# The second pointwise product of a conformer block: twelve of sixteen chunks by Strassen's seven products, with row sums on GpSimd

## The chip, the cores and the metric

The kernel runs on one core of one Trainium2 chip. The metric is the device time of one execution in microseconds; lower is better. The engines of a core are called by their names in the profile: PE (TensorE, with PEld for its weight loads), DVE (VectorE), ACT (ScalarE), POOL (GpSimd) and SP (SyncE, which issues most of the transfers).

## The reference

A conformer block over x of shape 2 x 4000 x 512 in bfloat16: a feed-forward layer, attention, a convolution module, a second feed-forward layer, with layer norms between. The part around the change is the end of the convolution module and what follows it.

```python
B, T, D = x.shape
...
h = _layernorm(x2, axis=-1)
h = h @ w_pw1
a = h[..., :D].copy()
b = h[..., D:].copy()
h = a * _sigmoid(b)
...                       # depthwise convolution over 3 tokens: dc
flat = dc.reshape(-1, D)
mu = flat.mean(0)
var = ((flat - mu) ** 2).mean(0)
dc = (dc - mu[None, None, :]) / jnp.sqrt(var[None, None, :] + 1e-05)
h = _silu(dc) @ w_pw2     # the second pointwise product
x3 = x2 + h
h = _layernorm(x3, axis=-1)
h = _silu(h @ w_ff2_a) @ w_ff2_b
x4 = x3 + 0.5 * h
return _layernorm(x4, axis=-1)
```

The second pointwise product multiplies each token's 512 values by the 512 x 512 matrix w_pw2, and its result is added to x2.

## The kernel before, in words

The tokens are worked on in 16 chunks (NCK) of up to 512, eight for each of the two sequences (TCB); the eighth of each has 416. A chunk has four token tiles of up to 128. The norm over all tokens inside the convolution module cuts the work in two: what follows it, called the second stage here, can start only when the convolution of all chunks is done. The second stage is a loop over c = 0 to 14 (`ff2`) and a last piece for chunk 15 (`ff_last`).

`ff2(c)` runs the second feed-forward layer of chunk c in 16 steps f (`ff_chunk`). Its two matrix products are done by Strassen's scheme, with matmuls of 128x256. Beside each step, `hook(f)` lays work for the chunks ahead: for chunk n = c + 2 (AHEAD is 2) the second pointwise product, for chunk n + 1 the silu that feeds it (`swish`, on ACT, into one of two buffers z), and the load of an x chunk (`get_x`). Layer norms of chunk c + 1 ("in") and of chunk c ("out") run as jobs beside them: statistics on DVE, a power on POOL, a small product on DVE, and the scaling on ACT.

The second pointwise product before is plain. At the steps f = 6, 8, 10 and 12 (8, 10, 12, 14 for c = 0) one token tile is done: `pw2` issues four matmuls of 128x512, one for each 128 of the 512 inputs, which add up in a bank of PSUM. Two steps later `pw2_residual` adds the bank to x in SBUF by one DVE scalar_tensor_tensor (xt<-y,xt in the profile). The bank comes from `sbank`, which is bank 7 in this stage. The results wait in x for the layer norm.

The x of a chunk lives in one of six homes of 4096 bytes per partition, called slots (SLOTS), and one chunk has a home of its own (TCB - 1). `slot(c, by)` names the home; `get_x` issues its load on SP's queue. The output of a chunk is stored from its home, also on SP's queue, and the home can be loaded again when that store is done. Before, `get_x(n + 1, ...)` stands at f = 8.

The order of the instructions on each engine is not the order of the code. The program collects its operations in a plan (`S.planned(16000, 8000)`), which holds costs for each operation and places them by a list schedule; `carry_out` then issues them engine by engine in that order. Almost all operations go through one helper, so the profile gives nearly all of them the same line, L93; they are told apart by engine, operation, tile names and shape. The tiles are named by their region: `xt` holds the x homes, `work`, `sums`, `keys` and `wff` are regions of SBUF with several uses each, `y` and `s` are banks of PSUM.

Of the kernel before, what the change touches and what calls it, by code (L numbers as in the profile page):

```python
# [5 lines left out]
F32 = mybir.dt.float32  # L6
BF16 = mybir.dt.bfloat16
I32 = mybir.dt.int32
ALU = mybir.AluOpType
# [6 lines left out]
TILE = 128  # L16
TPC = 4
CHUNK = TPC * TILE
# [3 lines left out]
NCK = B * TCB  # L22
# [7 lines left out]
HC, HD, HF = CHUNK // 2, D // 2, FC // 2  # L30
# [14 lines left out]
def token_tiles(c):  # L45

    return TPC if c < NCK - 1 else TPC - 1
# [510 lines left out]
class Conformer:  # L558
# [20 lines left out]

    IN = (1, 1, 2, 2, 3, 5, 5, 7, 9, 11)  # L580
    OUT = (5, 5, 9, 9, 10, 12, 13, 15, 17, 19)
    SOON = (5, 5, 9, 9, 10, 12, 12, 13, 14, 15)

    def __init__(self, nc, ins, out):
# [9 lines left out]
    def memory(self):  # L594
# [9 lines left out]
        E = Region(nc, "sums", 35840)  # L604
# [46 lines left out]
        at = [8192 + t % self.CONV_SLOTS * 4096 if t < self.NBESIDE else 20480 + (t - self.NBESIDE) * 4096  # L651
              for t in range(NCK)]
# [23 lines left out]
        def take(n):  # L676
# [6 lines left out]
                    for s in range(2)]  # L683
# [97 lines left out]
        self.b_zh = [[[C.buf("zh", o + cc * 2 * CHUNK + h * 2 * HC, 2 * HC) for h in range(2)] for cc in range(DC)]  # L781
                     for o in (oM, oQ0)]
        assert off[0] == 47104

        homes = ((C, oQ1), (E, 28672), (W, 8192))
        self.h2 = [[R.view(o + j * 1024, D) for j in range(TPC)] for R, o in homes]
# [1790 lines left out]
    def pw2(self, t, tiles, banks, start=True):  # L2577

        for ccs in (range(1), range(1, 2), range(2, 3), range(3, DC)) if len(tiles) > 1 else (range(DC),):
            for ti, (ps, b_ps) in zip(tiles, banks):  # L2580
                for cc in ccs:
                    self.mm(ps[0:TILE, :], self.z[t % 2][:, cc, ti * TILE:(ti + 1) * TILE], self.Wp2[:, cc, :],
                            start and cc == 0, cc == DC - 1,
                            [self.b_z[t % 2][cc] if t > 1 else self.b_zh[t][cc][ti // 2], self.b_Wp2], b_ps, inc=cc == ccs[-1])

    def pw2_residual(self, t, tiles, banks):
        for ti, (ps, b_ps) in zip(tiles, banks):
            self.residual(ps[0:TILE, :], b_ps, t * TPC + ti, 1.0)
# [53 lines left out]
    def program(self, any_score):  # L2642
# [50 lines left out]
        def ff1(c):  # L2693
# [26 lines left out]
            def done():  # L2720
                self.put_x(c)
                late = (self.SOON, (1, 1, 1, 1, 2, 2, 3, 3, 4, 4) if not any_score else (2, 2, 3, 3, 4, 6, 6, 6, 7, 7), (18, 18, 19, 19, 20, 22, 22, 23, 24, 25))
                self.ln_job(c, "key", "ACT", self.OUT if c < NCK - 3 else late[c - NCK + 3])

# [170 lines left out]
        x = [(ps[0:TILE, :], b_ps) for ps, b_ps in banks]  # L2895
# [8 lines left out]
        for k in range(2):  # L2904
# [3 lines left out]
            for ti in pair:  # L2908
# [3 lines left out]
                                                            in1=self.neghalf[0:TILE, two], op=ALU.pow),  # L2912
                 reads=self.b_mv[sl][two] + [self.b_neghalf], writes=self.b_rs[sl][two])
            S.op("DVE", lambda e, two=two: e.scalar_tensor_tensor(
                out=self.sh[sl][:, two], in0=self.mv[sl][:, two, 0], scalar=-1.0, in1=self.rs[sl][:, two],
# [8 lines left out]
        for h in range(2):  # L2924
            for f, (ps, b_ps) in enumerate(self.early):
                out = ps[:, h * HC:(h + 1) * HC].rearrange("p (t k) -> p t k", t=2)
                for cc in range(DC):
                    self.mm(out, self.Wa[:, cc, f * 128:(f + 1) * 128], self.lnT[0][:, 2 * h:2 * h + 2, cc, 0:TILE],
                            cc == 0 and h == 0, cc == DC - 1, [self.b_Wa[f * self.NWA // FC]] + self.b_lnT[0][2 * h:2 * h + 2],
                            b_ps, skip_group_check=True)  # L2930
        for ti in all_t:
            ps, b_ps = banks[ti]
            self.away("ACT", self.XT[ti], ps[0:TILE, :], b_ps, [self.bx[ti]], self.b_lnT[0])

        def ff2(c):
            def hook(f):
                n = c + AHEAD
                if f == 8 and n + 1 < NCK:
                    self.get_x(n + 1, self.slot(n + 1, 2))
                if c == 0 and f < 2:  # L2940
                    self.fetch_conv(3 + f)
                if c == 0 and f == 0:
                    for cc in range(DC):
                        self.swish(1, cc, 1, behind=self.b_lnT[0][0:1])
                if c == 0 and f in (2, 4):
                    ti = 1 + f // 2
                    bank = [self.sbank()]
                    self.pw2(1, [ti], bank)
                    self.after(1, lambda: self.pw2_residual(1, [ti], bank))
                if c == 0 and f in (2, 3, 5, 6):  # L2950
                    self.swish(n, (2, 3, 5, 6).index(f), behind=self.b_lnT[0][2:4])
                if c == 0 and f == 7:
                    self.fetch_conv(5)
                at = (8, 10, 12, 15) if c == 0 else (1, 5, 9, 13)
                if n + 1 < NCK and f in at:
                    self.swish(n + 1, at.index(f))
                if f == FC - 1 and c + 6 < self.NBESIDE:
                    self.fetch_conv(c + 6)
                times = (8, 10, 12, 14) if c == 0 else (6, 8, 10, 12)
                if n < NCK and f in times[0:token_tiles(n)]:  # L2960
                    ti = times.index(f)
                    bank = [self.sbank()]
                    self.pw2(n, [ti], bank)
                    self.after(2, lambda: self.pw2_residual(n, [ti], bank))
                if f == 0 and c + 1 < NCK:
                    if c:
                        self.ln_job(c + 1, "in", "ACT", self.IN)
                    else:
                        self.ln_job(1, "in", "ACT", (3, 4, 5, 7, 7, 8, 8, 8, 9, 9))

            def done():
                if c < NCK - 2:
                    self.ln_job(c, "out", "ACT", self.OUT)
                else:
                    self.ln_job(c, "out")

            self.ff_chunk(c, second, hook, done)

        self.fast, self.mixed = [c < NCK - 1 for c in range(NCK)], True
# [63 lines left out]
```

## Time and profile before

| | |
|---|---|
| median of 3 runs | 1875.03 us (1874.97 to 1876.97) |
| the profiled execution's own time | 1876.08 us |
| its span, first to last instruction | 1871.9 us |
| granted TensorE clock | 0.999 |
| PE busy | 1851.6 us (99%) |
| DVE busy | 1471.1 us (79%) |
| ACT busy | 1317.5 us (70%) |
| POOL busy | 135.4 us (7%) |
| second stage, steady chunks | about 1484 to 1791 us of the span |

Busy time is the time in which at least one instruction of the engine was running; for PE the ends of matmuls are modelled, since they overlap. The difference between the profiled execution's time and its span is what lies before the first and after the last instruction. A row of a group reads: line, engine, operation, written tile from read tiles, shape, count, then busy time and mean duration in ns, then the idle time of the engine just before these instructions and what ended most of it. A row of the timeline reads: start, duration, engine, line, operation, and in brackets the idle time before it.

### The profile page before, as it was taken

The page shows a single profiled execution, that of the slowest core. Times are in us where ns is not written, and L with a number is a line of the kernel's source. Part 1 is how long each engine was busy: PE and PEld are TensorE (multiplying, and loading weights), DVE is VectorE, ACT ScalarE, POOL GpSimd, SP SyncE. Part 2 cuts the span into 40 slices and gives each one's busy share as a digit, 9 for nine tenths or more (in the row PEclk, how much of TensorE's full clock was granted, in tenths as well). Part 3 has the DMA queues.
Part 4 walks back from the last instruction along what each step waited for, and adds up shares of the span by engine and source line. Part 5 has one row for each costly group of instructions (what it writes and reads, how often), then busy time and mean ns, then how long its engine had stood idle before and what let it go on. Part 6 is the DMA issues. An engine that isn't in the chain of part 4 may idle for free.

```text
span 1871.9 us, 39333 instructions
## 1 busy us (share of the span) xinstructions
PE 1851.6 (99%) x15370; PEld 1453.3 (78%) x15484; DVE 1471.1 (79%) x3212; ACT 1317.5 (70%) x2441; POOL 135.4 (7%) x302
## 2 busy tenths in 40 slices
PE   9999999999999999999999999999999999999998
PEld 6888888866777777777677777777775888888886
DVE  8888888868767777776777677767778988888875
ACT  6877777644666777777667676777668787777773
POOL 1000000000000000000000001000011000000000
PEclk9999999999999999999999999999999999999999
DMA  7333344297545555447955444444365222212111
GB/s 197 85 90 91 80 113 107 53 261 224 177 142 146 164 170 162 112 137 170 231 150 142 124 123 111 125 137 122 109 206 163 83 57 73 75 46 62 49 43 33
DMA packets 325014, 231.53 MB, mean 124 GB/s; under 512 B 204179, under 2 KB 295638, under 8 KB 324566
## 3 DMA queue, kind: packets, MB, share of 16 engines
q1 hardware_dynamic: 324294, 228.68, 44.4%
q8 instruction: 124, 2.03, 0.4%
q14 instruction: 68, 0.56, 0.1%
q10 hardware_dynamic: 528, 0.26, 0.0%
HBM read 128.44 MB, written 55.79 MB: 98 GB/s over the span
## 4 chain that ended last, share of the span: by engine, by line
PE 93%; DVE 2%; ACT 2%; DMA 1%; issue 1%; SPq 1%; DVEq 0%
PE y L93 48%; PE s L93 45%; ACT sums L93 1%; DVE work L93 1%; DVE xt L93 1%; SPq L93 1%; ACT work L93 0%; DMA kfd<-xt 0%; DVE sums L93 0%; DMA vhd<-wff 0%; DVE wff L93 0%; ACT wff L93 0%; ACT keys L93 0%; DMA wff<-keysd 0%; DMA work<-work 0%
## 5 line engine op out<-in xcount | busy, mean ns | idle before, releaser
L93 ACT ACTIVATE sums<-s 128x512 bf16<-128x512 f32 (+3 forms) x501 | 290.4, 584 | 112.2 <-PE s L93 108.4
L93 ACT ACTIVATE keys<-s 128x512 bf16<-128x512 f32 (+2 forms) x271 | 158.7, 588 | 176.0 <-PE s L93 158.1
L93 DVE TENSOR_TENSOR sums<-sums 128x512 bf16<-128x512 bf16 (+3 forms) x528 | 195.8, 397 | 67.8 <-ACT sums L93 62.8
L93 PE MATMUL y<-work,keys 128*128 128x256 bf16 x1920 | 244.2, 273 | 0.0
L93 PE MATMUL s<-work,keys 128*128 128x256 bf16 (+5 forms) x1430 | 219.8, 290 | 2.0 <-ACT sums L93 0.3
L93 ACT ACTIVATE work<-xt,work 128x512 bf16<-128x512 bf16 x268 | 208.0, 786 | 8.1 <-DVE work L93 7.9
L93 PE MATMUL y<-sums,keys 128*128 128x256 bf16 (+1 forms) x1440 | 212.3, 270 | 0.1
L93 PE MATMUL y<-wff,keys 128*128 128x256 bf16 (+2 forms) x1590 | 208.7, 276 | 0.4 <-DVE xt L93 0.4
L93 PE MATMUL s<-sums 128*128 128x256 bf16 x1380 | 206.1, 273 | 0.8 <-DVE sums L93 0.6
L93 PEld LDWEIGHTS y<-work,keys 128*128 128x128 bf16 x1920 | 187.8, 98 | 23.5 <-DVE work L93 0.2
L93 PE MATMUL y<-work,wff 128*128 128x256 bf16 (+3 forms) x1168 | 196.1, 291 | 0.0
L93 DVE TENSOR_TENSOR keys<-keys 128x1024 bf16<-128x1024 bf16 (+2 forms) x262 | 168.9, 663 | 27.9 <-ACT keys L93 14.7
L93 PEld LDWEIGHTS y<-wff,keys 128*128 128x128 bf16 (+1 forms) x1592 | 151.2, 98 | 31.5 <-issue 3.3
L93 DVE BATCH_NORM_STATS2 work<-xt 128x6 f32<-128x512 bf16 x251 | 163.8, 679 | 1.9 <-DMA xt<-in_x_dram 1.1
L93 PEld LDWEIGHTS s<-work,keys 128*128 128x128 bf16 (+1 forms) x1456 | 118.1, 97 | 56.0 <-ACT sums L93 5.9
L93 PEld LDWEIGHTS y<-sums,keys 128*128 128x128 bf16 x1440 | 137.1, 98 | 27.6 <-issue 6.1
L93 PEld LDWEIGHTS s<-sums 128*128 128x128 bf16 x1380 | 134.6, 98 | 23.9 <-DVE sums L93 0.8
L93 POOL TENSOR_TENSOR work<-work 128x4 f32<-128x4 f32 (+3 forms) x107 | 90.0, 842 | 806.8 <-DVE work L93 804.2
L93 PE MATMUL y<-sums,xt 128*128 128x256 bf16 (+1 forms) x960 | 146.2, 270 | 0.0
L93 PEld LDWEIGHTS y<-work,wff 128*128 128x128 bf16 x1168 | 113.0, 98 | 25.8 <-ACT s L93 0.4
L93 PE MATMUL s<-xt,keys 128*128 128x256 bf16 (+1 forms) x816 | 124.3, 270 | 0.8 <-DVE xt L93 0.7
L93 PE MATMUL s<-work 128*128 128x512 bf16 (+5 forms) x494 | 118.7, 376 | 5.3 <-DVE work L93 1.4
(143 smaller groups left out, 3227.4 us busy)
## 6 DMA issues: line engine op xcount, KB each, us to landing
xt<-kfd SPq DMA_DIRECT2D x98, 384.0 KB, 3.3
xt<-v12d SPq DMA_DIRECT2D x105, 256.0 KB, 2.7
xd<-xt SPq DMA_DIRECT2D x28, 512.0 KB, 2.9
xt<-xd SPq DMA_DIRECT2D x28, 512.0 KB, 4.3
out_dram<-xt SPq DMA_DIRECT2D x14, 512.0 KB, 3.1
xt<-in_x_dram SPq DMA_DIRECT2D x13, 512.0 KB, 4.4
dcvd<-wff SPq DMA_DIRECT2D x48, 128.0 KB, 2.1
keys<-dcvd SPq DMA_DIRECT2D x12, 512.0 KB, 3.7
```

The lines of the kernel that those rows point to most:

```text
L93: return getattr(eng, self.name)(*self.args, **self.kw)
```

## The change

For the chunks n = 3 to 14 (c = 1 to 12) the product of the chunk's 512 x 512 block with w_pw2 is done by the seven products of Strassen's scheme in its Winograd form, with blocks of 256 x 256, instead of eight.

- Each of the seven products is four matmuls of 128x256 into bank 7 (`pw2_unit`), at the steps f = 3, 5, 6, 8, 9, 11 and 13 (SEVEN). One DVE tensor_tensor one step later adds the bank to a block of x, or to a partial sum in 32-bit floats (`zt`), and writes either. Three of the seven start a bank afresh; four add to what the bank already holds, so some products accumulate across units.
- The four sums of rows (tokens) of z are POOL tensor_tensor operations of 128x512 in bfloat16, at f = 0 to 3 (`pw2_sums`); three go to new buffers `zs`, one overwrites a block of z.
- The four sums of weights are made once, at c = 0 and f = 12 to 15, by DVE operations of 128x512 (`pw2_weights`), and kept in `wz`.
- `wz` takes the place of the sixth home of x. In the second stage x goes through five homes (`slot(n, 2, 5)`), and `get_x(n, ...)` stands at f = 3 of the loop that also does the product of n, where it was at f = 8 of the loop before.
- Chunks 0, 1, 2 and 15 keep the plain product.

```diff
+    SEVEN = (3, 5, 6, 8, 9, 11, 13)
...
+        at = (self.SLOTS - 1) * 4096
+        self.wz = [self.XR.view(at + m * 1024, 512).rearrange("p (c d) -> p c d", c=2) for m in range(4)]
...
+    def pw2_weights(self, step):
+        (b11, b12), (b21, b22) = [[self.Wp2[:, 2 * k:2 * k + 2, e * HD:(e + 1) * HD] for e in range(2)] for k in range(2)]
...
+        out, x, y, op, rd, wr = ((t1, b12, b11, ALU.subtract, [], n1), (t3, b22, b12, ALU.subtract, [], n3),
+                                 (t2, t3, b11, ALU.add, n3, n2), (t4, b21, t2, ALU.subtract, n2, n4))[step]
+        self.S.op("DVE", lambda e: e.tensor_tensor(out=out, in0=x, in1=y, op=op), reads=rd + [self.b_Wp2], writes=wr)
+
+    def pw2_sums(self, t, step):
...
+        out, x, y, op, rd, wr = ((s1, a21, a22, ALU.add, b_z, n1), (s2, s1, a11, ALU.subtract, n1 + b_z[0:2], n2),
+                                 (s4, a12, s2, ALU.subtract, n2 + b_z[2:4], n4),
+                                 (a21, a11, a21, ALU.subtract, b_z[0:2], b_z[0:2]))[step]
+        self.S.op("POOL", lambda e: e.tensor_tensor(out=out, in0=x, in1=y, op=op), reads=rd, writes=wr)
+
+    def pw2_unit(self, t, n):
...
+        (form, b_f), (w, b_w), new, (x, b_x), (out, b_out) = (
+            (a12, b21, True, x11, p), (a11, b11, True, p, x11), (s2, t2, False, x12, p), (s3, t3, False, x22, q),
+            (a22, t4, False, x21, x21), (s1, t1, True, q, x22), (s4, b22, False, p, x12))[n]
+        ps, b_ps = self.bank(7)
+        for u in range(2):
+            for j in range(2):
+                self.mm(ps[0:TILE, u * HD:(u + 1) * HD], form[:, j, u * TILE:(u + 1) * TILE], w[:, j, :],
+                        new and u == 0 and j == 0, u == 1 and j == 1, b_f + [b_w], b_ps, skip_group_check=True)
+        y = ps[0:TILE, :].rearrange("p (t d) -> p t d", t=2)
+
+        def add():
+            self.S.op("DVE", lambda e: e.tensor_tensor(out=out, in0=y, in1=x, op=ALU.add), reads=[b_ps] + b_x, writes=b_out)
+
+        self.after(1, add)
...
                 n = c + AHEAD
-                if f == 8 and n + 1 < NCK:
-                    self.get_x(n + 1, self.slot(n + 1, 2))
+                if f == 3 and 0 < c and n < NCK:
+                    self.get_x(n, self.slot(n, 2, self.SLOTS - 1))
+                if c == 0 and f >= 12:
+                    self.pw2_weights(f - 12)
+                seven = 0 < c and n < NCK - 1
+                if seven and f < 4:
+                    self.pw2_sums(n, f)
+                if seven and f in self.SEVEN:
+                    self.pw2_unit(n, self.SEVEN.index(f))
...
-                if n < NCK and f in times[0:token_tiles(n)]:
+                if n < NCK and not seven and f in times[0:token_tiles(n)]:
```

More of the change, by code (lines that the diff above doesn't have):

```diff
@@ L783, in memory @@
         assert off[0] == 47104
+        self.zs = [E.view(28672 + m * 1024, 512).rearrange("p (c k) -> p c k", c=2) for m in range(3)]
+        self.b_zs = [E.buf("zs", 28672 + m * 1024, 1024) for m in range(3)]
+        self.zt = [E.view(31744 + m * 2048, CHUNK, F32).rearrange("p (t d) -> p t d", t=2) for m in range(2)]
+        self.b_zt = [E.buf("zt", 31744 + m * 2048, 2048) for m in range(2)]
+        at = (self.SLOTS - 1) * 4096
+        self.wz = [self.XR.view(at + m * 1024, 512).rearrange("p (c d) -> p c d", c=2) for m in range(4)]
+        self.b_wz = [self.XR.buf("wz", at + m * 1024, 1024) for m in range(4)]
         homes = ((C, oQ1), (E, 28672), (W, 8192))
@@ L2584, in pw2 @@
                             [self.b_z[t % 2][cc] if t > 1 else self.b_zh[t][cc][ti // 2], self.b_Wp2], b_ps, inc=cc == ccs[-1])
+    def pw2_weights(self, step):
+        (b11, b12), (b21, b22) = [[self.Wp2[:, 2 * k:2 * k + 2, e * HD:(e + 1) * HD] for e in range(2)] for k in range(2)]
+        t1, t2, t3, t4 = self.wz
+        n1, n2, n3, n4 = [[b] for b in self.b_wz]
+        out, x, y, op, rd, wr = ((t1, b12, b11, ALU.subtract, [], n1), (t3, b22, b12, ALU.subtract, [], n3),
+                                 (t2, t3, b11, ALU.add, n3, n2), (t4, b21, t2, ALU.subtract, n2, n4))[step]
+        self.S.op("DVE", lambda e: e.tensor_tensor(out=out, in0=x, in1=y, op=op), reads=rd + [self.b_Wp2], writes=wr)
@@ new lines, in pw2_sums @@
+    def pw2_sums(self, t, step):
+        z, b_z = self.z[t % 2], self.b_z[t % 2]
+        (a11, a12), (a21, a22) = [[z[:, 2 * k:2 * k + 2, h * HC:(h + 1) * HC] for k in range(2)] for h in range(2)]
+        s1, s2, s4 = self.zs
+        n1, n2, n4 = [[b] for b in self.b_zs]
+        out, x, y, op, rd, wr = ((s1, a21, a22, ALU.add, b_z, n1), (s2, s1, a11, ALU.subtract, n1 + b_z[0:2], n2),
+                                 (s4, a12, s2, ALU.subtract, n2 + b_z[2:4], n4),
+                                 (a21, a11, a21, ALU.subtract, b_z[0:2], b_z[0:2]))[step]
+        self.S.op("POOL", lambda e: e.tensor_tensor(out=out, in0=x, in1=y, op=op), reads=rd, writes=wr)
@@ new lines, in pw2_unit @@
+    def pw2_unit(self, t, n):
+        z, b_z = self.z[t % 2], self.b_z[t % 2]
+        (a11, a12), (s3, a22) = [[(z[:, 2 * k:2 * k + 2, h * HC:(h + 1) * HC], b_z[2 * k:2 * k + 2]) for k in range(2)]
+                                 for h in range(2)]
+        b11, b21, b22 = [(self.Wp2[:, 2 * k:2 * k + 2, e * HD:(e + 1) * HD], self.b_Wp2) for k, e in ((0, 0), (1, 0), (1, 1))]
+        s1, s2, s4 = [(x, [b]) for x, b in zip(self.zs, self.b_zs)]
+        t1, t2, t3, t4 = zip(self.wz, self.b_wz)
+        (x11, x12), (x21, x22) = [[(self.XTc[t][:, 2 * h:2 * h + 2, e * HD:(e + 1) * HD], self.bx[t * TPC + 2 * h:t * TPC + 2 * h + 2])
+                                   for e in range(2)] for h in range(2)]
+        p, q = [(x, [b]) for x, b in zip(self.zt, self.b_zt)]
+        (form, b_f), (w, b_w), new, (x, b_x), (out, b_out) = (
[10 more added lines that the diff above has]
+        self.after(1, add)
```

## The prediction

> **What bounds the kernel now.** The page comes first: the busy times by engine, and the chain that ended last.
>
> ```profile
> span 1871.9 us, 39333 instructions
> ...
> PE 1851.6 (99%) x15370; PEld 1453.3 (78%) x15484; DVE 1471.1 (79%) x3212; ACT 1317.5 (70%) x2441; POOL 135.4 (7%) x302
> ...
> PE 93%; DVE 2%; ACT 2%; DMA 1%; issue 1%; SPq 1%; DVEq 0%
> ```
>
> TensorE (PE) is busy nearly always and carries 93% of the chain. But a share over the whole span says little about one stage, so the second look is at the stage that is changed: the chain in order of time there, whose columns are start, duration, what.
>
> ```profile
> 1511.88 1.69 PE y L93 x11
> ...
> 1539.79 1.68 PE y L93 x11
> ...
> 1544.52 0.87 PE s L93 x8
> ...
> 1567.70 1.68 PE y L93 x11
> ```
>
> The same piece comes back at 1511.88, 1539.79 and 1567.70: one chunk of 512 tokens takes 27.91 us, and the pieces between are PE's. Eight matmuls of 128x256 take 0.87 us, 0.1088 each. The third look is at the engines by stretch (length, then busy time and count of PE, PEld, DVE, ACT, POOL, then clock, DMA share, GB/s).
>
> ```profile
> 1430.00:1460.00 30.00, 28.99 (x228) 21.70 (x230) 27.89 (x51) 26.19 (x47) 2.90 (x2) 1.00 0.31 89
> 1550.00:1580.00 30.00, 29.89 (x256) 24.97 (x257) 25.95 (x54) 22.25 (x40) 2.02 (x2) 1.00 0.29 71
> ```
>
> In the steady chunks PE has 29.89 of 30 us and waits for nobody; but VectorE (DVE) has 25.95 of 30, which is 24.1 us of each 27.91 us period. It is second by 3.8 us a chunk, no more. At the start of the stage (1430 to 1460) DVE is already nearly full and PE loses a little to it:
>
> ```profile
> PE s L93 <- DVE work L93: 1.6, 2, 1.0
> ...
> PE s L93 <- DVE sums L93: 0.6, 1, 0.6
> ```
>
> These are PE's waits for DVE between 1424 and 1484: 2.2 us in all.
>
> **What goes from PE.** The second pointwise product is seen in the timeline of one chunk (start, duration, engine, operation).
>
> ```profile
> 1543.49 1.03 PE L93 MATMUL y<-work 128*128 128x512 bf16 x4
> ...
> 1544.36 0.60 PE L93 MATMUL s<-sums 128*128 128x256 bf16 x4
> ...
> 1544.56 0.69 DVE L93 SCALAR_TENSOR_TENSOR xt<-y,xt 128x512 bf16<-128x512 f32 x1 [1.35 <-PE y L93]
> ...
> 1544.97 0.39 SPq L93 DMA_DIRECT2D out_dram<-xt  x1
> ...
> 1545.40 0.51 SPq L93 DMA_DIRECT2D xt<-xd  x1
> ```
>
> One token tile is four matmuls of 128x512; the next group starts 0.87 us later (1543.49 to 1544.36), so one costs 0.2175. A chunk has 16: 3.48 us. Seven products of four matmuls of 128x256 are 28 x 0.1088 = 3.05 us. Each of the 28 needs its own weight load instead of 16:
>
> ```profile
> L93 PEld LDWEIGHTS y<-wff,keys 128*128 128x128 bf16 x528 | 51.7, 98 | 8.3
> ...
> L93 DVE TENSOR_TENSOR keys<-keys 128x1024 bf16<-128x1024 bf16 x88 | 57.5, 684 | 7.9 <-ACT keys L93 7.6
> ...
> L93 DVE SCALAR_TENSOR_TENSOR xt<-y,xt 128x512 bf16<-128x512 f32 x55 | 37.7, 686 | 17.4 <-PE y L93 16.5
> ...
> L93 DVE TENSOR_TENSOR s<-s,sums 128x512 f32<-128x512 f32 x44 | 30.5, 694 | 2.3 <-PE s L93 2.3
> ...
> L93 POOL TENSOR_TENSOR work<-work 128x4 f32<-128x4 f32 x22 | 22.2, 1010 | 278.3 <-DVE work L93 278.3
> ...
> L93 DVE TENSOR_TENSOR sums<-work,sums 128x512 bf16<-128x512 bf16 x22 | 9.1, 414 | 0.0
> ```
>
> (These are groups by form over 11 chunks, 1484 to 1791: busy us and mean ns, then idle time before.) A load takes 98 ns, less than the 0.1088 us of its matmul, and other Strassen products run at that pace now, so loads stay hidden. PE saves 0.434 us a chunk, in 12 chunks (3 to 14) **5.2 us**. That is all there is to win: 0.28%. The measurement can tell about 0.2% (3.75 us) from no change, so nearly the whole gain must survive to be seen.
>
> **What DVE gets.** Four residuals a chunk at 686 ns go, seven additions from PSUM come; their nearest row is s<-s,sums, 694 ns, of the same kind. Operations that follow one another begin closer than their durations: three rows below stand at 1397.02 and 1397.67, 0.65 apart. So three more take 1.9 us: 24.1 + 1.9 = 26.0 us against a period that shrinks to 27.47. DVE goes from 86% to 95%. By the sum PE still bounds, with 1.5 us of room a chunk.
>
> The four weight sums are made once, in chunk 0 of the stage, 0.414 us each: 1.7 us on DVE, where it was busy 27.89 of 30. Between nothing (they fit in the 2.1 us of gaps) and 1.7; I take **0.2**, as the gaps are as large as the work.
>
> **The new waits of PE.** All seven products go through one PSUM bank (7): a product waits until the addition of the one before has read the bank. In the order in which the instructions are issued, before has one place a steady chunk where a matmul needs a DVE operation that stands only eight matmuls (0.87 us) ahead; with DVE's 0.69 us that leaves 0.18 us. After has mostly three such a chunk, of which two wait for bank 7. Besides, in chunks c=3 and c=5 one has no matmul between (short by up to 0.69 us), and in c=1, 11 and 12 one has four (0.44 us, short by 0.25): 2 x 0.69 + 3 x 0.25 = 2.1 us if DVE is just on time, nothing if DVE runs ahead of its place. I take **1.0**, the middle.
>
> **GpSimd and the port.** Four row sums a chunk move to GpSimd (POOL). It has two of exactly this form in the whole run:
>
> ```profile
> L93 POOL TENSOR_TENSOR wff<-wff 128x512 bf16<-128x512 bf16 x2 | 2.3, 1156 | 0.0
> ```
>
> So 4 x 1.16 = 4.6 us a chunk beside 2.02 in 30 now: POOL has time. Between a sum and the matmul that reads it stand other matmuls worth some 14 us (3.5 us in c=1); that wait alone costs nothing. What is queued behind them on POOL is the power for the layer norm (1.01 us, twice a chunk); in the steady chunks it stands over 40 matmuls (4 us) behind the last sum, so it is not late. The question is what POOL does to DVE. One of the two sums shows it:
>
> ```profile
> 1397.02 0.73 DVE L93 SCALAR_TENSOR_TENSOR xt<-s,work,xt 128x512 bf16<-128x512 f32 x1
> 1397.67 0.58 DVE L93 SCALAR_TENSOR_TENSOR work<-work 128x1 f32<-128x1 f32 x1
> ...
> 1397.08 1.16 POOL L93 TENSOR_TENSOR wff<-wff 128x512 bf16<-128x512 bf16 x1
> ...
> 1400.41 0.14 DVE L93 SCALAR_TENSOR_TENSOR work<-work 128x1 f32<-128x1 f32 x1
> ```
>
> The POOL sum runs from 1397.08 to 1398.24. The DVE operation that reads PSUM and one operand in SBUF (1397.02) is not slowed. The tiny one with two SBUF operands, 0.14 us at 1400.41, takes 0.58 at 1397.67: it ends at 1398.25, just when POOL is done. It was held up for 0.44 us. The Trainium skill, page "SBUF — State Buffer", section "Who interferes with whom", calls this an exclusive lock: a DVE instruction with two SBUF inputs and a GpSimd instruction that reads SBUF block each other for the whole instruction, whoever comes first. The rows agree, and the rule speaks against this change.
>
> Exposed are the eight keys<-keys sums of 684 ns and the four sums<-work of 414 ns a chunk. The seven new additions, having one PSUM operand, are not. In a steady chunk the order puts the first POOL sum beside an addition from PSUM, and three keys<-keys sums in a row 1.2 us later, beside the second POOL sum. Bounds for one chunk: nothing (DVE gets the port first, POOL waits and has time), or three stops that alternate with POOL's, 2.65 us. Nearest is the one seen, 0.44. Of that the tight matmul absorbs 0.18, so PE would lose 0.26; DVE is packed from there to the next tight matmul. I take it in every second chunk: 6 x 0.26 = **1.6 us**. Below nothing it cannot go.
>
> **Five homes for x.** A chunk's load now goes to the home whose output store was issued three chunks before, and in a few chunks it waits for that store.
>
> ```profile
> out_dram<-xt SPq DMA_DIRECT2D x14, 512.0 KB, 3.1
> ...
> xt<-xd SPq DMA_DIRECT2D x28, 512.0 KB, 4.3
> ```
>
> Store to landing 3.1, issue 0.5 (1545.40), load 4.3: 7.9 us. In chunks 5, 6, 13 and 14 about 12 us lie between the issue of the store and the first addition that reads x; elsewhere 18. Loads already stand right behind stores on SP's queue (1544.97, 1545.40). Cost nothing; if the 4 us of cover went, the bank-7 chain and so PE would wait the rest.
>
> **Sum.** 5.2 - 1.0 - 1.6 - 0.2 = 2.4 us. The profiled run took 1876.08 us (its span 1871.9 and 4.2 around it): 1873.7. It stands 1.05 above the median of the runs, 1875.03, so in terms of the median **1872.6 us**: 0.13% less, within what can be told from no change. Its own range is 1870.8 to 1875.
>
> **Rivals.**
> *The gain stays whole.* POOL finds the port between DVE's operations, and DVE, which waits for the product in 16.5 us of 11 chunks (the xt<-y,xt row), runs ahead of its places. For it: PE waits for nobody in the steady chunks now. Then 1875.03 - 5.2 = 1869.8, with some tenths lost 1870.3.
>
> *DVE becomes the bound.* The place is each chunk's stretch with POOL's sums beside the keys<-keys sums; the price is the lock. 26.0 us plus D of blocking reaches the old period of 27.91 at D = 1.9, under two whole POOL sums; at 2.65 the chunk takes 28.65, 0.74 more than now, times 12: +8.9, 1883.9. PE needs to lose only 0.434 us a chunk for the kernel to be slower. For it: a tenth of DVE's room is left, and four sums a chunk try for the port. Against: in the steady chunks only one or two of the four stand beside DVE work with two SBUF operands. In c=1 to 4 and from c=10 on more do.
>
> *The loads of x or POOL's power come late.* Late by 2 us in each of the four close chunks, PE waits 8 us: 1880.6. Against: the cover above. That the change doesn't do what it says is hardly open: the matmuls fall from 16 x 512 to 28 x 256 columns in 12 chunks.
>
> **How the numbers follow.** Forecast 0.40 (a fifth of it, 0.08, below 1871.3, where faster begins), the whole gain 0.28, DVE as the bound 0.24 (0.20 of it above 1878.8, 0.04 below), late loads or powers 0.08, all slower. Faster 0.36, same 0.36, slower 0.28. The range goes from the whole gain, 1869.4, with a little for the pace, to near the lock's upper end, 1883, since the unknown is the lock.
>
> **What would show it.** The chunk's period should come to about 27.7 us from 27.91; a stretch of 30 us in the steady chunks should show DVE at 28 or more and POOL at about 7. PE's waits in the steady chunks, none now, should appear as waits for DVE of some 0.2 us a chunk, at y matmuls of 128x256 (bank 7). The keys<-keys group's mean should rise from 684 ns if the lock costs DVE; POOL's 128x512 sums would show more than 1156 ns if DVE wins the port instead. I am wrong if PE's waits for DVE come to over 5 us in all, or if PE waits for a DMA in this stage, or if the group's mean is unchanged and PE yet waits.

## The result and the profile after

The changed kernel takes 1895.41 us (median of 5 runs, 1892.79 to 1896.78), the kernel before in the same comparison 1875.18: 20 us slower, ratio 1.010 (95% interval 1.0089 to 1.0110). The prediction said 1872.6 with 1869.4 to 1883.0: wrong, in size and in direction.

The profiled execution of the changed kernel is the shortest of the five, 1892.79 us; its span is 1888.6. First its page: the span, the busy times, the chain that ended last.

```profile
span 1888.6 us, 39872 instructions
...
PE 1858.1 (98%) x15628; PEld 1464.4 (78%) x15628; DVE 1508.4 (80%) x3250; ACT 1323.7 (70%) x2443; POOL 198.7 (11%) x350
...
PE 84%; DVE 10%; ACT 3%; issue 2%; DMA 1%; POOL 0%; DVEq 0%; SPq 0%; ACTq 0%
```

The span grew by 16.7 us. On the chain, PE fell from 93% to 84% and DVE rose from 2% to 10%. GpSimd, which got the new work, is at 0%: the engines' shares alone would not make a reader suspect it. Next come the two stretches of the prediction (length, then PE, PEld, DVE, ACT, POOL, then clock, DMA share, GB/s).

```profile
1430.00:1460.00 30.00, 26.83 (x208) 19.69 (x206) 27.15 (x47) 25.45 (x44) 8.09 (x6) 0.99 0.31 75
...
1550.00:1580.00 30.00, 28.61 (x261) 24.95 (x259) 27.37 (x52) 22.39 (x38) 8.82 (x7) 1.00 0.25 46
```

PE has 28.61 of 30 us in the steady chunks where it had 29.89, and DVE is not full: 27.37. The start of the stage lost 2.2 us of PE (28.99 to 26.83). SP's transposes, one set a chunk, give the chunk's period:

```profile
1600.58 5.13 SPq L93 DMA_TRANSPOSE work<-work  x4
...
1687.24 5.13 SPq L93 DMA_TRANSPOSE work<-work  x4
```

Three chunks in 86.66 us: 28.89 us a chunk, against 27.91 before and the 27.47 that PE's work alone would need. Some rows of the waits between 1520 and 1790 (in total, times, longest), where PE waited for nobody before:

```profile
PE y L93 <- ACT keys L93: 3.9, 6, 0.8
PE y L93 <- DVE work L93: 3.5, 8, 1.1
...
PE y L93 <- DVE sums L93: 1.6, 1, 1.6
```

PE's four rows that name DVE come to 6.0 us there; the prediction had named 5 us as the sign of being wrong.

Then the groups by form (1490 to 1820), which had 684 ns, 414 ns and, for GpSimd's sums, 1156 ns before:

```profile
L93 DVE TENSOR_TENSOR keys<-keys 128x1024 bf16<-128x1024 bf16 x92 | 73.3, 811 | 1.9 <-ACT keys L93 1.9
...
L93 POOL TENSOR_TENSOR sums<-work,sums 128x512 bf16<-128x512 bf16 x10 | 15.0, 1497 | 2.7 <-PE y L93 2.6
...
L93 DVE TENSOR_TENSOR sums<-y,xt 128x512 f32<-128x512 f32 x32 | 21.8, 681 | 6.6 <-PE y L93 6.4
...
L93 DVE TENSOR_TENSOR sums<-work,sums 128x512 bf16<-128x512 bf16 x24 | 12.3, 514 | 0.0
```

The means of DVE's sums of two SBUF operands rose (684 to 811, 414 to 514 ns), and so did that of GpSimd's (1156 to 1497). Not every sum became longer: counted one by one in the trace, 16 of the 92 keys<-keys sums took 0.83 to 1.65 us, and the other 76 kept 0.64 to 0.69. The new additions from PSUM take 681 ns, undisturbed. The timeline of one chunk shows what happens to the longer ones:

```profile
1644.81 1.16 POOL L93 TENSOR_TENSOR sums<-work 128x512 bf16<-128x512 bf16 x1 [9.37 <-PE s L93]
1645.39 4.24 DVE L93 TENSOR_TENSOR keys<-keys 128x1024 bf16<-128x1024 bf16 x3
1646.04 1.48 POOL L93 TENSOR_TENSOR sums<-sums,work 128x512 bf16<-128x512 bf16 x1
1647.60 1.48 POOL L93 TENSOR_TENSOR work<-work 128x512 bf16<-128x512 bf16 x1
1649.05 1.60 POOL L93 TENSOR_TENSOR sums<-work,sums 128x512 bf16<-128x512 bf16 x1
```

Three keys<-keys sums in a row should take 1.9 us and take 4.24. One by one they show that the two engines take turns:

```profile
1645.39 1.12 DVE L93 TENSOR_TENSOR keys<-keys 128x1024 bf16<-128x1024 bf16 x1
...
1646.43 1.64 DVE L93 TENSOR_TENSOR keys<-keys 128x1024 bf16<-128x1024 bf16 x1
...
1647.99 1.64 DVE L93 TENSOR_TENSOR keys<-keys 128x1024 bf16<-128x1024 bf16 x1
```

DVE's second sum stands from 1646.43 and ends at 1648.07, 0.55 us after GpSimd's (1646.04 + 1.48 = 1647.52); GpSimd's next, begun at 1647.60, ends 1.0 us after that. From the second on, each waits until the other's instruction is done, and each held sum of DVE takes 0.95 us longer. Four chunks, from 1616 to 1705, have three such sums in a row; in the first four of the twelve chunks no keys<-keys sum is held up, only the small ones (sums<-work, 0.41 us to as much as 1.37). The chain in order of time shows what follows from it:

```profile
1645.47 1.10 DVE keys L93 x2
1646.57 1.42 issue
1647.99 1.64 DVE keys L93
...
1650.84 1.19 DVE xt L93 x2
...
1654.40 2.06 DVE work L93 x7
...
1660.18 1.05 PE y L93 x8
```

From 1642 to 1660 the chain lies on DVE, which works off its delay one operation behind the other, and only at 1660 does PE carry it again. ("issue" at 1646.57 is the hold-up itself.)

### The profile page after: what moved, and what is told of

It reads as the page before. It is cut to its first block, busy times and chain, and to the rows that moved or that the text cites. A ratio compares the mean times of both kernels' runs of the same rounds, so it can differ in the third digit from the quotient of the medians.

```text
span 1888.6 us, 39872 instructions
## 1 busy us (share of the span) xinstructions
PE 1858.1 (98%) x15628; PEld 1464.4 (78%) x15628; DVE 1508.4 (80%) x3250; ACT 1323.7 (70%) x2443; POOL 198.7 (11%) x350
## 4 chain that ended last, share of the span: by engine, by line
PE 84%; DVE 10%; ACT 3%; issue 2%; DMA 1%; POOL 0%; DVEq 0%; SPq 0%; ACTq 0%
PE s L93 43%; PE y L93 41%; DVE work L93 3%; DVE keys L93 2%; DVE sums L93 2%; DVE xt L93 2%; ACT work L93 1%; DVE s L93 1%; DMA work<-work 1%; ACT keys L93 1%; ACT xt L93 0%; ACT sums L93 0%; POOL work L93 0%; DVE wff L93 0%; DMA xt<-in_x_dram 0%
## 5 line engine op out<-in xcount | busy, mean ns | idle before, releaser
L93 PE MATMUL s<-work,keys 128*128 128x256 bf16 (+5 forms) x1456 | 224.9, 292 | 0.5 <-ACT sums L93 0.3
L93 PE MATMUL y<-wff,keys 128*128 128x256 bf16 (+3 forms) x1592 | 209.2, 276 | 1.2 <-DVE xt L93 1.1
L93 DVE TENSOR_TENSOR keys<-keys 128x1024 bf16<-128x1024 bf16 (+2 forms) x262 | 181.9, 707 | 22.6 <-PE s L93 10.1
L93 POOL TENSOR_TENSOR work<-work 128x4 f32<-128x4 f32 (+4 forms) x119 | 107.5, 905 | 668.1 <-DVE work L93 664.5
L93 PE MATMUL s<-work 128*128 128x512 bf16 (+4 forms) x545 | 128.0, 373 | 3.0 <-DVE work L93 3.0
```

Source lines behind the costliest of these rows:

```text
L93: return getattr(eng, self.name)(*self.args, **self.kw)
```

## The experiments

Since the first 1391 to 1394 us of the program are the same in all and differ by up to 3.1 us between the profiled executions, the table also gives the length of the rest in the profiled execution: from the piece of eight matmuls s<-work,wff of 128x512 that starts at 1391.34 in the kernel before, to the end of the span.

| kernel | median us | ratio to before (95%) | rest of the profile, us |
|---|---|---|---|
| before | 1875.2 to 1876.7 | | 480.6 |
| the change | 1895.41 | 1.0089 to 1.0110 | 497.4 |
| 1 no row sums | 1875.44 | 0.9988 to 1.0007 | 477.8 |
| 2 row sums on DVE | 1873.10 | 0.9973 to 0.9993 | 476.1 |
| 3 row sums later | 1888.65 | 1.0050 to 1.0083 | 491.3 |
| 4 five homes and weight sums, plain product | 1878.01 | 1.0002 to 1.0021 | 482.1 |
| 5 row sums on DVE, from c = 2 | 1872.05 | 0.9974 to 0.9992 | 475.4 |
| 6 five homes only | 1876.30 | 0.9995 to 1.0013 | 481.2 |
| 7 weight sums only | 1878.04 | 1.0002 to 1.0021 | 479.8 |
| 8 memset for the row sums | 1875.67 (one run) | | 480.3 |
| 9 plain product with row sums | 1896.53 | 1.0086 to 1.0119 | 501.0 |

The rests hold one thing more. In the stretches from 1400 to 1460 the granted clock was below 1.00 in some of the profiled executions: 0.94 in one of the two stretches in the kernel before and in experiments 3, 4, 6 and 8, 0.90 and 0.99 in the change, 0.92 and 0.96 in experiment 9, and 1.00 in 1, 2, 5 and 7. At 30 us a stretch that is up to 1.8, 3.3, 3.6 and 0 us of PE's time (an estimate). No run here shows whether the changes cause it.

**1. No row sums.**

```diff
-                if seven and f < 4:
-                    self.pw2_sums(n, f)
...
-        s1, s2, s4 = [(x, [b]) for x, b in zip(self.zs, self.b_zs)]
+        s1, s2, s4 = s3, a11, a12
```

> The changed kernel with the four row sums of each chunk left out; the seven products read blocks of z in their place, so PE, DVE and the transfers have the same work and GpSimd has none of the new work. Theory lock (GpSimd's row sums and DVE's keys<-keys sums hold each other up): most of the 20 us come back, 1871 to 1876 us, the keys<-keys group's mean is 684 ns again, and the chunk takes 27.5 to 27.7 us. Rival additions (seven additions through one bank make PE wait for DVE whatever GpSimd does): still 1886 or more, with PE's waits for DVE in the steady chunks as they are. Rival homes (five homes and the weight sums cost at the start and in the loads): 1890 or more.

Measured 1875.44: the 20 us are gone with four instructions a chunk that nobody sees on the chain. In the steady chunks PE is full (30.00 of 30 in each stretch from 1580 to 1790) and the keys<-keys mean is 681 ns. The rival "additions" is out. From the page:

```profile
PE 1846.0 (99%) x15539; PEld 1466.0 (78%) x15628; DVE 1489.0 (80%) x3250; ACT 1322.2 (71%) x2443; POOL 134.8 (7%) x302
```

The same 3250 instructions of DVE keep it busy for 1489.0 us, where the change has 1508.4: the hold-ups made DVE's work 19.4 us longer. By its median this run only equals the kernel before, though 5.2 us less is asked of PE. By the rest of the profile it wins 2.8 us. Part of what is missing is lost at the start of the stage, where PE has 28.35 us between 1430 and 1460 (28.99 before); the remainder is not explained.

**2. Row sums on DVE.**

```diff
-        self.S.op("POOL", lambda e: e.tensor_tensor(...), reads=rd, writes=wr)
+        self.S.op("DVE", lambda e: e.tensor_tensor(...), reads=rd, writes=wr)
```

> The row sums on DVE instead of GpSimd, nothing else. DVE gets 4 x 0.41 = 1.7 us more a chunk and nothing can hold it up. Theory lock: DVE needs about 26.0 + 1.7 = 27.7 us a chunk, so it is full but the chunk stays near 27.9: 1874 to 1882 us, faster than the change by 12 us or more. Rival additions: DVE was the trouble without GpSimd, so more work on it makes it worse than the change, 1898 or more.

Measured 1873.10, faster than before by 0.17%, and better than expected. (It also lies below experiment 1, which gives DVE less to do; the intervals of the two overlap.) The stretch and the chain (1520 to 1790):

```profile
1640.00:1670.00 30.00, 30.00 (x278) 26.88 (x276) 29.03 (x61) 23.59 (x41) 2.10 (x2) 1.00 0.21 54
```

```profile
by line: PE y L93 68.2%; PE s L93 31.9%; issue 0.0%
```

DVE is busy 29.03 of 30 us, and yet the chain is PE's alone. So a full DVE does not cost PE anything here; the same four sums cost 22 us more (1895.41 less 1873.10) on GpSimd, which is idle for most of the time. The chunk takes 27.51 us (1598.44 to 1680.97 in three), the 27.47 that PE's work needs.

```profile
1598.44 1.19 SPq L93 DMA_TRANSPOSE work<-work  x1
...
1680.97 1.19 SPq L93 DMA_TRANSPOSE work<-work  x1
```

**3. Row sums later on GpSimd.**

```diff
-                    self.pw2_sums(n, f)
+                    self.pw2_sums(n, f, [b[0] for b in second.b_s] if f == 0 else [])
...
-        self.S.op("POOL", ..., reads=rd, writes=wr)
+        self.S.op("POOL", ..., reads=rd + behind, writes=wr)
```

> The first row sum of a chunk also waits for the last of the four keys<-keys sums of the first half of the chunk before (its result is named as read); the row sums stay on GpSimd, with the same work on every engine, only some 4 us later, beside DVE operations that read PSUM or one operand in SBUF. Theory lock: in the steady chunks the keys<-keys mean falls from 811 ns to about 690, GpSimd's sums take 1.16 us again, and the time is 1873 to 1881 us; what is left is the start of the stage. Rival additions: no change, 1892 to 1897. If GpSimd slows every DVE operation, not only those with two operands in SBUF, also 1892 or more.

Measured 1888.65: a third of the loss comes back, and the expected 1873 to 1881 is missed. The timeline of a steady chunk shows that the step itself does what it should:

```profile
1644.24 1.89 DVE L93 TENSOR_TENSOR keys<-keys 128x1024 bf16<-128x1024 bf16 x3
...
1646.56 1.16 POOL L93 TENSOR_TENSOR sums<-work 128x512 bf16<-128x512 bf16 x1 [12.74 <-DVE keys L93]
1646.65 0.69 DVE L93 BATCH_NORM_STATS2 work<-xt 128x6 f32<-128x512 bf16 x1
...
1647.80 1.16 POOL L93 TENSOR_TENSOR sums<-sums,work 128x512 bf16<-128x512 bf16 x1
1647.84 0.68 DVE L93 TENSOR_TENSOR xt<-y,sums 128x512 bf16<-128x512 f32 x1
```

The keys<-keys sums take 1.89 again and GpSimd's 1.16, beside DVE operations with one operand in SBUF that keep their 0.68. In the chunks between 1610 and 1730 PE is full. Elsewhere the sums meet other DVE work with two operands in SBUF, and PE loses as before:

```profile
1520.00:1550.00 30.00, 28.39 (x259) 24.86 (x257) 27.53 (x57) 23.30 (x42) 8.78 (x7) 1.00 0.26 71
...
1640.00:1670.00 30.00, 30.00 (x277) 26.89 (x275) 27.37 (x57) 23.76 (x41) 6.62 (x6) 1.00 0.20 54
```

and the group of the small sums (1490 to 1790) has a mean of 601 ns, where 414 is undisturbed:

```profile
L93 DVE TENSOR_TENSOR sums<-work,sums 128x512 bf16<-128x512 bf16 x21 | 12.6, 601 | 0.0
```

**4. Five homes and the weight sums, plain product.**

```diff
-                seven = 0 < c and n < NCK - 1
+                seven = False
```

> Five homes for x, the load at its new place and the weight sums as in the change, but the plain second product in all chunks, so none of the seven products and no row sums. Theory lock and rival additions: 1875 to 1877 us, as before. Rival homes: a good part of the 20 us is here, 1880 or more, with PE waiting at the start of the stage or for x.

Measured 1878.01, 0.02 to 0.21% slower than before: a little over the 1877 that two of the theories allowed, and no place for 20 us. In the profile PE waits for no transfer.

**5. Row sums on DVE, from c = 2.** Experiment 2 with the weight sums one chunk later.

```diff
-                if c == 0 and f >= 12:
+                if c == 1 and f >= 12:
...
-                seven = 0 < c and n < NCK - 1
+                seven = 1 < c and n < NCK - 1
```

> Row sums on DVE as in the second experiment, and the weight sums one chunk later (c = 1 instead of 0), so that the seven products are used from c = 2: eleven chunks instead of twelve. The start of the stage, where DVE is full, then has the work of before. Theory: 11 x 0.434 = 4.8 us from PE, and the start costs nothing more: 1870 to 1872 us, 1 to 3 us below the second experiment. If the loss at the start is not the sums' but that of the five homes, it stays: 1873 to 1875.

Measured 1872.05, at the upper end of the expected 1870 to 1872; faster than before by 0.08 to 0.26%, and the shortest rest of all. That it is better than experiment 2 by 1 us can't be told from these intervals.

**6 and 7. Five homes only, weight sums only.** The sixth leaves out the weight sums of experiment 4; the seventh keeps them (into the space of `zt`, which the plain product leaves free) and has six homes and the load as before.

> The plain product in all chunks and no weight sums: only the five homes and the new place of the load. If the 1.5 us of the fourth experiment's stage come from the homes: the stage is 482 us again and the time about 1877. If from the weight sums: as before, stage 480.6, 1875 to 1876.

> The plain product in all chunks, six homes and the load as before, and only the four weight sums added at c = 0 (into a buffer that the plain product leaves free). The other half of the same question: 1877 and a stage of 482 us if the weight sums are what costs, 1875 to 1876 and 480.6 if the homes are.

Measured 1876.30 (not told from before) and 1878.04 (0.02 to 0.21% slower). By the medians the weight sums cost and the homes do not; but the profiled executions say 481.2 and 479.8, the other way. The one of the seventh was its fastest run (1874.99), with a clock of 1.00 from 1400 to 1430 where the sixth has 0.94 (up to 1.8 us). So the medians point to the weight sums, and it is not settled.

**8. Memset for the row sums.**

```diff
-        self.S.op("POOL", lambda e: e.tensor_tensor(out=out, in0=x, in1=y, op=op), reads=rd, writes=wr)
+        self.S.op("POOL", lambda e: e.memset(out, 1.0), reads=rd, writes=wr)
```

> The changed kernel with each of GpSimd's row sums replaced by a memset of the same tile, with the same waits: GpSimd writes what the products read, but reads nothing from SBUF. Theory lock: it is GpSimd's reading that holds up DVE's sums of two SBUF operands, so the keys<-keys mean is 684 ns and the time 1870 to 1878 us. If any GpSimd work beside DVE slows it, the keys<-keys mean stays above 720 ns and the time above 1880.

Measured 1875.67 in one run, keys<-keys mean 683 ns. The timeline has a memset in the middle of three keys<-keys sums:

```profile
1661.71 1.89 DVE L93 TENSOR_TENSOR keys<-keys 128x1024 bf16<-128x1024 bf16 x3
1661.98 0.52 POOL L93 MEMSET work<- 128x512 bf16 x1
```

Neither is held up. So GpSimd's work as such is harmless here; what is left as the cause is its reading of SBUF beside DVE's sums of two operands. Two reservations: a memset takes 0.52 us, not 1.16, and one wait of PE for a DVE sum that the change has (1.6 us, once) is here too, with 1.7 us, so that one is not shown to come from the hold-up.

**9. Plain product with row sums.** Experiment 4, with the row sums into a buffer that nobody reads, behind the first keys<-keys sum (the fourth sum's result goes to `zs` too).

```diff
-                if seven and f in self.SEVEN:
+                if False and f in self.SEVEN:
...
-                    self.pw2_sums(n, f)
+                    self.pw2_sums(n, f, second.b_s[0][0:1] if f == 0 else [])
```

> The plain second product in all chunks, as in the fourth experiment, and beside it GpSimd's four row sums a chunk into a buffer that nobody reads, started behind the first of the four keys<-keys sums, so that they run beside the other three. DVE has 24.1 us of work in a chunk of 27.91 here, so there is room for a hold-up of 2.4 us. If the hold-up costs only where DVE has no room in a chunk (a bound by throughput): as the fourth experiment, 1877 to 1880 us, with a keys<-keys mean near 800 ns. If it costs where it happens, because matmuls need a DVE result soon after: 0.5 to 1.3 us a chunk, 1884 to 1894 us.

Measured 1896.53, 18.5 us over experiment 4 and a little worse than the second theory allowed. No product reads these sums, PE's work is that of before, and DVE has room. The timeline, a stretch, SP's transposes, and two rows of the waits between 1520 and 1790:

```profile
1647.28 4.32 DVE L93 TENSOR_TENSOR keys<-keys 128x1024 bf16<-128x1024 bf16 x3
```

```profile
1670.00:1700.00 30.00, 29.04 (x246) 23.83 (x247) 26.03 (x49) 22.21 (x39) 7.38 (x6) 1.00 0.19 54
```

```profile
1541.33 6.39 SPq L93 DMA_TRANSPOSE work<-work  x4
...
1774.96 6.41 SPq L93 DMA_TRANSPOSE work<-work  x4
```

```profile
ACT keys L93 <- DVE sums L93: 22.2, 18, 1.9
...
PE y L93 <- ACT keys L93: 6.8, 9, 0.8
```

Three sums take 4.32 us instead of 1.89. Eight chunks take 233.63 us, 29.20 each, against 27.91 before; DVE is busy for 26.0 us of each (208.2 in the eight), hold-up included, so it is not full, and would not be in 27.91 either. So the hold-up costs where it happens. Part of how it reaches PE is in the last two rows: a late DVE sum makes a silu on ACT late (keys), and a matmul waits for that. No row of the waits has an engine waiting for a result of GpSimd.

## Why the prediction was wrong

**PE's saving: right.** Experiment 2 has the chunk of 27.51 us against the 27.47 worked out; the additional weight loads cost nothing that shows there.

**DVE's additions and room: right in kind.** The additions take 681 ns. DVE's load was overrated: 29.03 of 30 with the row sums on it is 26.6 us of 27.51, a microsecond less than 26.0 + 1.7, so there was more room than the sum had, not less.

**Bank 7 and the near places: 1.0 us taken, none found in the steady chunks.** With DVE 97% busy, in experiment 2, PE waits for nobody between 1520 and 1790.

**Weight sums: 0.2 us taken, not settled.** Experiment 7 gives 0.4 to 3.9 us by its interval, and its profile's rest gives nothing.

**Five homes: nothing taken, nothing told apart** (experiment 6).

**Late loads or powers: not the cause.** In the change, PE waits for no transfer between 1520 and 1790, and DVE waits 4.2 us for GpSimd's power. It waits 2.4 us for it in experiment 1, without the 20 us, and not at all in experiment 9, with a loss as large.

**GpSimd and the port: the step that failed.** The mechanism was named, with the right row, and so was one of the places, three keys<-keys sums beside GpSimd's second. The size was not: 0.44 us of hold-up in every second chunk, 2.6 us in all, of which 1.6 were charged to PE. The runs show 19.4 us of hold-up on DVE (1508.4 less 1489.0) and, by the rests of the change (497.4) and of experiment 1 (477.8), about 20 us in time, of which up to 3.3 can be the clock. Two choices in it were bad. First, the value was taken from the nearest row, but that row is one tiny operation between two waits, which can be held up only once, and it was taken for half of the chunks. Three sums in a row, against four that are queued on the other engine with nothing between, are held up each time: by 2.35 us (4.24 less 1.89) in the chunk shown, where the upper bound of 2.65 us had just this count. And the small sums, which the prediction listed as exposed, are held up in other chunks. Second, the upper end of the time, 1883, came from adding the hold-up to DVE's busy time and asking whether the sum exceeds the period: 28.65 us a chunk. The chunk came out at 28.89, but experiment 9 shows that the question was wrong: DVE's 26.0 us leave room in the old period of 27.91, and PE loses 1.3 us a chunk all the same. The range also priced the steady chunks alone; between 1430 and 1490 the change has 2.4 us less of PE than experiment 1 (55.60 against 58.02). The rival *DVE becomes the bound* named the right cause and direction, and its 1883.9 us was still 11.5 us short.

The page "SBUF — State Buffer" of the Trainium skill, section "Who interferes with whom", calls the port pair that the two engines share an exclusive lock, and says that a DVE instruction with two SBUF inputs contends with a GpSimd instruction that reads SBUF, not with one that only writes it. The timeline and experiment 8 agree with both (4.24 us and 1.89 us for the same three sums). The prediction weighed the rule and then gave it the weight of a single case.

## What to carry to other kernels

Before moving elementwise work from a nearly full DVE to an idle GpSimd, count how many DVE instructions with two SBUF operands the order puts beside it, and price each one at nearly a whole GpSimd instruction (here 0.95 us beside sums of 1.16): back to back on both sides they take turns. Judge a delay by what waits for that engine's next results, not by the room it has in a period. Here the "full" engine was the better place: DVE at 97% cost PE nothing, GpSimd at a quarter cost 1%.

## What the runs showed of the hardware

- GpSimd's sum of 128x512 in bfloat16 takes 1.16 us undisturbed and up to 1.64 beside DVE's sums of two SBUF operands, which go from 0.68 to as much as 1.65 each; DVE takes 0.41 us for the sum that GpSimd takes 1.16 for.
- DVE operations that read PSUM and one SBUF operand, and the layer norm's statistics, keep 0.68 us beside the same GpSimd sums.
- A GpSimd memset of the same tile takes 0.52 us and holds up no DVE sum (means of 683 and 419 ns in experiment 8).
- A hold-up costs time although DVE has room: 29.20 us a chunk in experiment 9 with DVE busy for 26.0 of it.
